# Softmax divisors of the last two head groups taken through small f32 matmuls, and the last quarter's output sums held open in PSUM

## The chip, the cores and the metric

The kernel runs on one core of a Trainium2 chip. The core has five engines with instruction streams of their own: TensorE (PE in the profile; PEld is its weight loads), VectorE (DVE), ScalarE (ACT), GpSimd (POOL) and SyncE (SP), which issues the DMAs. They meet through semaphores. The metric is the device time of one execution in microseconds: 742.52 us for the kernel before, the median of three runs (740.91 to 743.12).

## The reference

One sequence of S = 2048 tokens of width D = 640 is layer-normalized. On the result, multi-query attention (H = 32 query heads of width 20, one shared key and value head) and a feed-forward network (width F = 1728, silu) run side by side; their sum is added to the input.

```python
xn = _layernorm(x)                                    # x: [1, 2048, 640] bf16
q = (xn @ wq) -> [B, H, S, 20];  k = xn @ wk;  v = xn @ wv
p = softmax(einsum("bhqd,bkd->bhqk", q, k) * 20 ** -0.5)
att = einsum("bhqk,bkd->bhqd", p, v) -> [B, S, 640] @ wo
ffn = silu(xn @ w1) @ w2
return x + att + ffn
```

## The kernel before

**Tiling.** The queries are taken in four quarters of 512 (`QC`), the heads in eight groups of four (`HG`), which makes 32 groups in all, numbered 0 to 31; groups 24 to 31 are the last quarter. A group works on 16 key tiles of 128. One score tile (one key tile, one head, 512 queries) is one PE matmul on one of four row groups (L894) into one PSUM bank. There are 2048 of them. Most are exponentiated on ACT, two or three banks in one instruction (L978, 671 instructions). The rest go in batches of four heads to DVE, which builds an approximate exponential out of integer arithmetic: one conversion per head (L1155, 576) and two shifts per batch (L1188).

**Values and divisors.** The exponentials are multiplied with `v_all` by four matmuls, one on each of four column groups of PE ("a set", L1010), into bank 7 (`UB`). Each head has 32 rows there: 20 of output and, in row 20, the softmax divisor, which comes from a constant column in `v_all`. When a group is done, bank 7 is copied to `U_sb` (L1056 on DVE; for group 31 on ACT in two halves, L1067). For groups 0 to 29, `norm_job` then spreads the 4x512 divisors by DMA to 128x16, inverts them on DVE (L717), spreads the result by further DMAs over the rows of each head, multiplies on POOL (L725) and packs the heads into `oT` by DMA.

**The last two groups** (30 and 31) have no time for DMAs. There `sum_job` multiplies `U_sb` by a selection matrix `sel_f`, which repeats each head's divisor over its 32 rows (an f32 matmul, L838), DVE inverts all 128 rows (L841) and multiplies (L843). Their output rows stay in the padded layout of 32 rows a head, and `wo_end` holds the matching rows of `wo`. `make_sel` builds `sel_f` on POOL in a slot of `qT` that is free after group 22.

**Output.** The out projection and the second FFN product of a tile of 128 tokens and half the width (320) accumulate in one bank: 14 FFN chunks and five chunks of `oT`, each a set of four matmuls on column groups (`col_mm`, L379). For the last quarter this is split. `y_job` does the FFN part early, for token tiles 2 and 3 with the first three chunks of `oT` (`YC`), and evicts with the residual to `yx` (L783). For tiles 0 and 1, `ya_job` does those three chunks as a sum of its own, evicted onto `yx` by DVE (L794). At the end eight `fin_job`s (four tiles, two halves: "fins") take the fourth chunk and group 30 ("finA"), then group 31 ("finB", `fin_b`), and DVE writes the result (L823), which is stored by a DMA per token tile (L753).

**Order.** The program is written out by a planner, not by hand. `build` keeps a clock for every engine with estimated costs, commits one operation after another, and `emit` turns the order of each engine into its instruction stream with the semaphore waits. So the order is fixed; what takes longer on the chip than in the plan makes the engine wait. A DMA's estimate is its size argument divided by 250 bytes per ns, behind the DMAs already under way (`Sched.commit`). Side work for PE stands in two lists: `misc`, in order, paced by `misc_total` against the progress of the attention, and `misc_front`, which goes first. `next_misc` takes from `misc_front` only its first entry. A fin may start when no `y` or `ya` is left in `misc` and group 30 is divided.

**Head.** The 16 tiles of x are loaded by `load_x` (L405), in order with `wk`, the first columns of `wq`, `wv` and the rest of `wq`. DVE takes statistics (L484, L486), POOL the power -0.5 (L493), DVE or POOL normalizes (L509, L506), PE transposes (L516), and keys (L542), values (L566) and queries (L589) follow. For tiles 6 and 7 ACT takes the statistics (L473, L475). The first exponential needs the keys of tile 0 and the queries of tiles 0 to 3.

Of the kernel before, what the change touches and what calls it, by code (L numbers as in the profile page):

```python
# [14 lines left out]
P = 128  # L15
# [58 lines left out]
YA = 3  # L74
# [194 lines left out]
def build(nc, A_x, A_wq, A_wk, A_wv, A_wo, B_x, B_w1, B_w2, out, stack):  # L269
# [41 lines left out]
    sel_f = qT[:, 2, 0:2 * P].bitcast(F32)  # L311
# [9 lines left out]
    rS = Rrep  # L321
# [18 lines left out]
    h0f = hT[0][:, :, :].rearrange("p a b -> p (a b)")  # L340
    yx = h0f[:, 0:2 * QTP * D].bitcast(F32).rearrange("p (t d) -> p t d", t=QTP)
# [61 lines left out]
    def load_x(n):  # L403
        r = [res("xres", n)] if n < QTP else []
        x_ld[n] = dma(f"x{n}", lambda e, n=n: e.dma_start(x_home[n], xv[:, n, :]), P * D * 2,  # L405
                      writes=[res("xr", n)] + r)
# [39 lines left out]
    d_wv = dma("wv", lambda e: e.dma_start(wv_sb[:, :, 0:DH], wrow(A_wv)), P * DC * 256, writes=[res("wv")])  # L446
    d_wq = dma("wq", lambda e: e.dma_start(wq_sb[:, :, :], wrow(A_wq)), D * D * 2, writes=[res("wqs")])
# [342 lines left out]
    def ya_job(qc, i, hf):  # L790

        e0, e1 = hf * HALF, (hf + 1) * HALF
        job = pe_job(f"ya{qc}_{i}_{hf}", o_mms(qc, i, e0, e1, True, True, range(YA)), YA * 140)
        op = Op("dve", lambda v: v.scalar_tensor_tensor(out=yx[:, i, e0:e1], in0=bk(job.bank, 0, HALF), scalar=0.5,  # L794
                                                        in1=yx[:, i, e0:e1], op0=ALU.mult, op1=ALU.add),
                t_dve(HALF), 140, pre=[job.ready, y_op[(i, hf)]], reads=[], writes=[res("yx", i, hf)], prio=0.3, job=job)
        y_op[(i, hf)] = op
        job.consumers = [op]
        return job

# [4 lines left out]
    def fin_job(qc, i, hf):  # L805
        e0, e1 = hf * HALF, (hf + 1) * HALF
        mms = o_mms(qc, i, e0, e1, True, False, range(YA, DC - 1))

        def fa(pe, b):
            return col_mm(pe, b, e1 - e0, oT[:, 1 - qc % 2, 1, i * P:(i + 1) * P], wo_end[:, 0, e0:e1], False, False)  # L810
        mms.append((fa, t_mc(e1 - e0), "p", [oT_op[(1, 0)]] + d_wo_end, [res("oT", "end", 1, 0)]))
        job = pe_job(f"fin{qc}_{i}_{hf}", mms, len(mms) * 140)
        job.ready = None
        n = QTP * qc + i
        sl = n % 3 if n < NT - 1 else "x"

        def com(op):
            if (qc, i, 0) in half_op and (qc, i, 1) in half_op:
                store(qc, i)
        args = dict(pre=[y_op[(i, hf)]] + ([y_op[(0, 0)], y_op[(0, 1)]] if sl == "x" else []), reads=[res("yx", i, hf)],  # L820
                    writes=[res("os", sl) if hf == 0 else res("os2", sl)] + ([res("xres", 0)] if sl == "x" else []), prio=0.3, job=job, on_commit=com)
        dst = stage(n)[:, e0:e1]
        op = Op("dve", lambda v: v.scalar_tensor_tensor(out=dst, in0=bk(job.bank, 0, HALF), scalar=0.5, in1=yx[:, i, e0:e1],  # L823
                                                        op0=ALU.mult, op1=ALU.add), t_dve(HALF), 140, **args)
        op.gate = lambda: job.ready is not None and (sl not in store_op or store_op[sl].done or (qc, i, 1 - hf) in half_op)
        op.on_commit = lambda o: (half_op.__setitem__((qc, i, hf), op), com(o))
        job.consumers = [op]
        fin_made[(i, hf)] = job
        return job
# [3 lines left out]
    def sum_job(g, lo, hi, uc, rd):  # L833

        us, e, n = g % 2, NGR - 1 - g, hi - lo

        def f(pe, b):
            return pe.matmul(bk(b, 0, n), sel_f, U_sb[:, us, lo:hi], start=True, stop=True)  # L838
        job = pe_job(f"sum{g}", [(f, 4 * n / 2.4, "f", [uc] + sel, rd)], 500)
        rw = [res("Rrep", h) for h in range(HG)]  # L840
        r = Op("dve", lambda v: v.reciprocal(rS[:, lo:hi], bk(job.bank, 0, n)), t_dve(n), 140, pre=[job.ready], writes=[res("rS", k) for k in range(lo * 2 // QW, hi * 2 // QW)] + (rw if e else []),  # L841
               prio=0.1, job=job)
        op = dve(lambda v: v.tensor_tensor(oT[:, 0, e, lo:hi], U_sb[:, us, lo:hi], rS[:, lo:hi], ALU.mult), t_dve(n), 140,  # L843
                 pre=[r] + [out_done[(QC - 2, t)] for t in range(QTP)], reads=rd + [res("rS", k) for k in range(lo * 2 // QW, hi * 2 // QW)], writes=[res("oT", "end", e, lo)], prio=0.1)
        job.consumers = [r]
        oT_op[(e, lo)] = op
        return job
# [198 lines left out]
    def end_group(g, pv):  # L1046
# [8 lines left out]
        if g < NGR - 1:  # L1055
# [3 lines left out]
            if g < NGR - 2:  # L1059
                norm_job(g, uc)  # L1060
            else:
                misc_front.append(("sum", g, 0, QW, uc, [res("U", us)]))
            return
        h = QW // 2
        for k in range(2):
# [3 lines left out]
            misc_front.insert(k, ("sum", g, lo, hi, uc, [res("Uh", k)]))  # L1069
        for f in fins:  # L1070
            if f not in fin_asked:
                misc_front.append(("finA", qc) + f)
            misc_front.append(("finB", qc) + f)
# [187 lines left out]
    def make_sel():  # L1261
        v = sel_f.rearrange("p (i r) -> p i r", r=SLOT)
        a = pool(lambda g: g.memset(sel_f, 0.0), 180, writes=q_res[NGR - NQ] + [res("sel")], prio=0.91)
        sel.append(pool(lambda g: g.affine_select(out=v, in_=v, compare_op=ALU.not_equal, fill=1.0, base=-DH,
                                                  pattern=[[-SLOT, HG], [0, SLOT]], channel_multiplier=1), 280, pre=[a],
                        reads=[res("sel")], writes=[res("sel")], prio=0.92))
# [9 lines left out]
    def fill_misc():  # L1276
# [17 lines left out]
        for i in range(QTP):  # L1294
            for hf in range(2):
                if YC[i] < YA:
                    misc.append(("ya", QC - 1, i, hf))

    fill_misc()
    COST = {"q": 1.1, "h": 1.2, "out": 2.7, "y": 2.2, "ya": 0.5}  # L1300
# [20 lines left out]
    MAKE = {"q": q_job, "h": h_job, "out": out_job, "y": y_job, "ya": ya_job, "sum": sum_job, "finA": fin_a, "finB": fin_b}  # L1321

    def ready_to_make(m):
        if m[0] == "out":
            return (m[1], NG - 1) in pack_op and (m[1], m[2]) in xres_op
        if m[0] == "ya":
            return (m[2], m[3]) in y_op and all((m[1], g) in pack_op for g in range((YA * P - 1) // (HG * DH) + 1))
        if m[0] == "sum":
            return all((QC - 2, t) in out_done for t in range(QTP))
        if m[0] == "finA":  # L1330
            return (m[2], m[3]) in y_op and not any(isinstance(x, tuple) and x[0] in ("y", "ya") or isinstance(x, Piece) for x in misc) and all((m[1], g) in pack_op for g in range(NG - 2)) and (1, 0) in oT_op
        if m[0] == "finB":
            return (m[2], m[3]) in fin_made and len(oT_op) == 3
# [50 lines left out]
    def next_misc():  # L1384
# [3 lines left out]
        for q, src, ahead in ((misc_front, "front", 1), (misc, "misc", 16)):  # L1388
# [390 lines left out]
```

## Time and profile before

| what | us |
|---|---|
| median of three runs | 742.52 (740.91 to 743.12) |
| profiled execution, its own time | 744.36 |
| its span | 742.50 |
| first exponential on ACT starts | 14.23 |
| last exponential on ACT ends | 727.10 |
| last matmul set of bank 7 for group 31, end of its step in the chain | 727.88 |
| divisors of group 31 inverted on DVE (two instructions of 128x256) | 729.08 to 732.45 |
| last output half evicted by DVE | 739.71 to 740.20 |
| ACT busy in the span | 710.6 (96%) |
| PE busy / DVE busy in the span | 709.3 (96%) / 659.2 (89%) |

The span reaches from the first to the last instruction of the profiled execution; that execution's own time is 1.86 us longer, and was not one of the three runs of the median. "Busy" counts instructions in work, and matmul ends are modelled, so a busy PE may still wait. In a table of stages each line has the stage, its length, then for PE, PEld, DVE, ACT and POOL the busy time and the number of instructions, and at the end the granted clock of PE, the DMA share and GB/s. In a timeline a line has the start, the length, the engine, the source line, the operation with its form (out<-in), the count and, in brackets, the engine's idle time before it with what ended it.

### The profile page before, as it was taken

How to read it: one execution, taken by the hardware profiler on the slowest of the kernel's cores; microseconds unless marked ns; L12 is line 12 of the kernel's file. 1: busy time of each engine (PE TensorE's matmuls, PEld its weight loads, DVE VectorE, ACT ScalarE, POOL GpSimd, SP SyncE). 2: the span in 40 equal slices, each digit the busy share in tenths (PEclk: the TensorE clock that was granted, in tenths of full speed). 3: DMA queues.
4: the chain of work that ended last, by engine and by line, in shares of the span. 5: the costliest groups of instructions: out<-in, count | busy, mean ns of one | idle time of the engine just before them, and what ended most of it. 6: DMA issues, size and time to landing. Idle time of an engine off the chain costs nothing.

```text
span 742.5 us, 22537 instructions
## 1 busy us (share of the span) xinstructions
PE 709.3 (96%) x9922; PEld 236.7 (32%) x9925; DVE 659.2 (89%) x1144; ACT 710.6 (96%) x745; POOL 62.4 (8%) x72
## 2 busy tenths in 40 slices
PE   7999999999999999999999999999999999999986
PEld 5422222222223333222223333322223333333333
DVE  7779999999999489899998997999989968798985
ACT  6999999999999999999999999999999999999892
POOL 5500000000010000000000000000000000000000
PEclk9999999999999999999999999999999999999999
DMA  8812211222221122322111222122222211232201
GB/s 215 300 28 26 19 17 22 29 28 28 18 19 24 30 29 30 68 29 25 18 14 26 32 30 33 19 64 25 28 21 20 27 18 20 39 56 22 18 5 37
DMA packets 34160, 28.89 MB, mean 39 GB/s; under 512 B 15470, under 2 KB 29582, under 8 KB 34062
## 3 DMA queue, kind: packets, MB, share of 16 engines
q1 hardware_dynamic: 34062, 27.45, 23.9%
q8 instruction: 78, 1.28, 0.7%
q14 instruction: 20, 0.16, 0.1%
HBM read 11.01 MB, written 2.62 MB: 18 GB/s over the span
## 4 chain that ended last, share of the span: by engine, by line
ACT 62%; PE 23%; DVE 11%; SPq 1%; DMA 1%; issue 1%; POOL 0%; DVEq 0%; POOLq 0%
ACT sbt L978 60%; PE psall L894 8%; PE psall L1010 7%; PE psall L379 7%; DVE sbt L1155 4%; DVE sbt L1188 3%; ACT sbt L655 2%; DVE sbt L841 1%; SPq L626 1%; DMA sbt<-in_A_x_dram 1%; PE psall L1433 1%; DVE sbt L658 1%; DVE sbt L486 0%; DVE sbt L484 0%; DVE sbt L823 0%
## 5 line engine op out<-in xcount | busy, mean ns | idle before, releaser
L978 ACT ACTIVATE sbt<-psall 128x1024 bf16<-128x1024 f32 (+1 forms) x671 | 685.9, 1221 | 10.7 <-PE psall L894 10.4
L1155 DVE TENSOR_SCALAR sbt<-psall 128x512 int16<-128x512 f32 x576 | 373.0, 679 | 13.6 <-PE psall L894 10.3
L894 PE MATMUL psall<-sbt 32*128 32x512 bf16 x2048 | 279.6, 385 | 14.4 <-ACT sbt L978 6.1
L1010 PE MATMUL psall<-sbt 128*32 128x512 bf16 x3200 | 254.3, 386 | 3.9 <-DVE sbt L1056 3.4
L379 PE MATMUL psall<-sbt 128*32 128x320 bf16 (+1 forms) x3944 | 242.9, 334 | 5.8 <-DVE sbt L841 1.9
L1188 DVE TENSOR_SCALAR sbt<-sbt 128x2048 int16<-128x2048 int16 x288 | 199.5, 709 | 15.9 <-PE psall L1010 15.2
L894 PEld LDWEIGHTS psall<-sbt 32*128 32x128 bf16 x2048 | 73.1, 91 | 265.9 <-ACT sbt L978 182.9
L379 PEld LDWEIGHTS psall<-sbt 128*32 128x32 bf16 x3944 | 86.2, 96 | 99.2 <-issue 58.2
L1010 PEld LDWEIGHTS psall<-sbt 128*32 128x32 bf16 x3200 | 66.2, 95 | 112.3 <-issue 74.6
L725 POOL TENSOR_TENSOR sbt<-sbt 128x512 bf16<-128x512 f32 x30 | 40.9, 1364 | 620.9 <-DVE sbt L1155 216.4
L658 DVE SCALAR_TENSOR_TENSOR sbt<-sbt,psall 128x512 bf16<-128x512 bf16 (+1 forms) x56 | 37.9, 676 | 2.9 <-ACT sbt L655 1.8
L655 ACT ACTIVATE sbt<-psall 128x512 bf16<-128x512 f32 (+1 forms) x56 | 39.2, 701 | 0.3 <-PE psall L379 0.3
L1433 PE MATMUL psall<-sbt 128*32 128x512 bf16 (+1 forms) x512 | 34.9, 353 | 1.2 <-DVE sbt L408 1.2
L768 DVE SCALAR_TENSOR_TENSOR sbt<-psall,sbt 128x320 bf16<-128x320 f32 x24 | 11.7, 488 | 25.0 <-PE psall L379 24.9
L1056 DVE COPY sbt<-psall 128x512 f32<-128x512 f32 x31 | 21.1, 681 | 0.4 <-PE psall L1010 0.3
L613 DVE TENSOR_SCALAR sbt<-psall 128x512 bf16<-128x512 f32 x20 | 13.6, 679 | 4.4 <-PE psall L379 4.3
L1433 PEld LDWEIGHTS psall<-sbt 128*32 128x32 bf16 x512 | 13.3, 104 | 12.0 <-issue 6.6
L516 PE MATMUL psall<-sbt 128*128 128x128 bf16 x80 | 7.5, 221 | 2.3 <-DVE sbt L509 1.7
L506 POOL TENSOR_SCALAR sbt<-sbt 128x640 bf16<-128x640 bf16 x10 | 9.0, 910 | 3.0 <-DVE sbt L498 2.4
L841 DVE RECIPROCAL sbt<-psall 128x256 f32<-128x256 f32 (+1 forms) x3 | 6.7, 2267 | 2.2 <-PE psall L838 2.2
L783 DVE SCALAR_TENSOR_TENSOR sbt<-psall,sbt 128x320 f32<-128x320 f32 x8 | 3.9, 485 | 5.2 <-PE psall L379 5.1
L484 DVE BATCH_NORM_STATS2 sbt<-sbt 128x6 f32<-128x320 bf16 x14 | 6.5, 470 | 2.0 <-DMA sbt<-in_A_x_dram 1.9
(53 smaller groups left out, 86.3 us busy)
## 6 DMA issues: line engine op xcount, KB each, us to landing
sbt<-sbt SPq DMA_DIRECT2D x120, 64.0 KB, 3.8
sbt<-in_A_x_dram SPq DMA_DIRECT2D x28, 160.0 KB, 3.4
sbt<-sbt SPq DMA_DIRECT2D x213, 20.0 KB
out_dram<-sbt SPq DMA_DIRECT2D x16, 160.0 KB, 1.9
sbt<-in_B_w_dram SPq DMA_DIRECT2D x1, 2160.0 KB, 11.7
sbt<-in_B_w_dram SPq DMA_DIRECT2D x1, 2080.0 KB, 15.6
sbt<-sbt SPq DMA_DIRECT2D x75, 8.0 KB
sbt<-in_A_wq_dram SPq DMA_DIRECT2D x1, 800.0 KB, 7.1
```

Source lines behind the costliest of these rows:

```text
L379: ins = pe.matmul(ps[j * SLOT:(j + 1) * SLOT, b * BANK:b * BANK + n], w[:, j * SLOT:(j + 1) * SLOT], x, start=start, stop=stop, tile_posit ...
L655: t = Op("act", lambda a: a.activation(t_buf[0:rows, ts, :], bk(job.bank, 0, QW, rows=rows), AF.Tanh, scale=0.5), t_act(512), 215, pre=[jo ...
L658: u = Op("dve", lambda v: v.scalar_tensor_tensor(out=hT[par][0:rows, fk, :], in0=t_buf[0:rows, ts, :], scalar=1.0, in1=bk(job.bank, 0, QW, ...
L725: nm = pool(lambda e: e.tensor_tensor(oU[:, us, :], U_sb[:, us, :], Rrep, ALU.mult), 1700, pre=[uc] + lc, reads=[res("U", us)] + [res("Rre ...
L841: r = Op("dve", lambda v: v.reciprocal(rS[:, lo:hi], bk(job.bank, 0, n)), t_dve(n), 140, pre=[job.ready], writes=[res("rS", k) for k in ra ...
L894: return pe.matmul(bk(b), kT_rep[i * SLOT:(i + 1) * SLOT, kt * P:(kt + 1) * P], qT[i * SLOT:(i + 1) * SLOT, g % NQ, :], start=True, stop=T ...
L978: return a.activation(Ebuf[:, es * QW:es * QW + w], ps[:, buf[0] * BANK:buf[0] * BANK + w], AF.Exp, scale=ESCALE)
L1010: ins = pe.matmul(ps[i * SLOT:(i + 1) * SLOT, UB * BANK:UB * BANK + QW], lhsT, rhs, start=(first and k < HG), stop=(last and k >= len(lst) ...
L1056: uc = Op("dve", lambda v: v.tensor_copy(U_sb[:, us, :], bk(UB)), t_dve(512), 140, pre=[pv] + up, reads=[sc.banks[UB]], writes=[res("U", u ...
L1155: p1 = Op("dve", lambda v: v.tensor_scalar(z16[:, i * QW:(i + 1) * QW], bk(job.bank), ZBIAS, 0.0, ALU.add, ALU.max), t_dve(QW), 140, pre=[ ...
L1188: op = dve(lambda v, t=t, j=j: v.tensor_scalar_add(t[:, :].bitcast(I16), z16, float(SHIFT[j])), t_dve(N, 4), prio=3.0 - 0.01 * j, **args)
L1433: ins = pe.matmul(ps[i * SLOT:(i + 1) * SLOT, UB * BANK:UB * BANK + n], zero_t[:, 0:SLOT], zero_t[:, 0:n], start=fresh, stop=fresh, tile_p ...
```

## The change

Three things change.

1. For groups 30 and 31 the divisors are inverted in a narrow layout. `sum_job` makes four f32 matmuls, one for each 128 queries, with `U_sb` as the weights and a selection matrix of four columns (`sel4`) as the moving operand: 128 queries lie on the partitions, and the divisors of all four heads and four query tiles fill 128x16. DVE inverts these into `rLg`. The new `spread_job` brings them back: for each query tile and head one f32 matmul on one of the four column groups, with one column of `rLg` repeated 32 times as weights and an identity matrix (`ident_e`) as the moving operand. DVE multiplies `U_sb` by the result in PSUM. For group 31 the spread and the product come in two halves of 256 queries. `make_sel` builds both matrices in the same slot.
2. `ya_job` is gone. The fins take all chunks of `oT` that their `y` left out (`range(YC[i], DC - 1)`): four for token tiles 0 and 1, one for tiles 2 and 3. The last two fins (`LATE`) wait for both halves of group 31, `misc_front` is searched 20 entries deep, and finB follows directly behind its finA in that list. A branch with an eviction on ACT and an addition on POOL is there too, but `FIN_ACT` is empty, so it is not used.
3. The size arguments of the first loads in the planner (not the DMAs themselves) are set one by one: x4 counts as 612500 bytes, x5 to x7 as 75000, x8 to x15 as 107500 (163840 before), `wv` as 25000 (163840 before) and `wq` as 475000 (819200 before).

```diff
-YA = 3
+LATE = 2
+FIN_ACT = ()
+T_SUM = 110.0
+T_SPREAD = 230.0
...
-    sel_f = qT[:, 2, 0:2 * P].bitcast(F32)
+    sel4 = qT[:, 2, 0:2 * HG].bitcast(F32)
+    ident_e = qT[:, 2, QW - 2 * P:QW].bitcast(F32)
...
-        x_ld[n] = dma(f"x{n}", lambda e, n=n: e.dma_start(x_home[n], xv[:, n, :]), P * D * 2,
+        x_ld[n] = dma(f"x{n}", lambda e, n=n: e.dma_start(x_home[n], xv[:, n, :]), P * D * 2 if n < 4 else 612500 if n == 4 else 75000 if n < 8 else 107500,
...
-    d_wv = dma("wv", lambda e: e.dma_start(wv_sb[:, :, 0:DH], wrow(A_wv)), P * DC * 256, writes=[res("wv")])
-    d_wq = dma("wq", lambda e: e.dma_start(wq_sb[:, :, :], wrow(A_wq)), D * D * 2, writes=[res("wqs")])
+    d_wv = dma("wv", lambda e: e.dma_start(wv_sb[:, :, 0:DH], wrow(A_wv)), 25000, writes=[res("wv")])
+    d_wq = dma("wq", lambda e: e.dma_start(wq_sb[:, :, :], wrow(A_wq)), 475000, writes=[res("wqs")])
...
-    def ya_job(qc, i, hf):
...
-        mms = o_mms(qc, i, e0, e1, True, False, range(YA, DC - 1))
+        mms = o_mms(qc, i, e0, e1, True, False, range(YC[i], DC - 1))
...
-    def sum_job(g, lo, hi, uc, rd):
...
-            return pe.matmul(bk(b, 0, n), sel_f, U_sb[:, us, lo:hi], start=True, stop=True)
-        job = pe_job(f"sum{g}", [(f, 4 * n / 2.4, "f", [uc] + sel, rd)], 500)
...
-        r = Op("dve", lambda v: v.reciprocal(rS[:, lo:hi], bk(job.bank, 0, n)), t_dve(n), 140, pre=[job.ready], ...
+    def sum_job(g, ucs):
+
+        us = g % 2
+        mms = []
+        for t in range(QTP):
+            uc, rd = ucs[t * len(ucs) // QTP]
+
+            def f(pe, b, t=t):
+                return pe.matmul(bk(b, t * HG, (t + 1) * HG), U_sb[:, us, t * P:(t + 1) * P], sel4, start=True, stop=True)
+            mms.append((f, T_SUM, "f", [uc] + sel, [rd]))
+        job = pe_job(f"sum{g}", mms, 500)
+        r = Op("dve", lambda v: v.reciprocal(rLg[:, us, :], bk(job.bank, 0, QTP * HG)), 230, 140, pre=[job.ready],
+               writes=[res("rLg", us)], prio=0.1, job=job, name="recip")
...
+    def spread_job(g, lo, hi, ucs):
+
+        us, e = g % 2, NGR - 1 - g
+        mms = []
+        for t in range(lo // P, hi // P):
+            def f(pe, b, t=t):
+                for j in range(HG):
+                    w = rLg[:, us, t * HG + j:t * HG + j + 1]
+                    ins = pe.matmul(ps[j * SLOT:(j + 1) * SLOT, b * BANK + t * P:b * BANK + (t + 1) * P],
+                                    bass.AP(rLg, w.offset, [list(w.ap[0]), [0, SLOT]]), ident_e, start=True, stop=True,
+                                    tile_position=(0, j * SLOT))
+                return ins
+            mms.append((f, T_SPREAD, "f", [recip_op[g]] + sel, [res("rLg", us)]))
+        job = pe_job(f"spread{g}", mms, 500)
+        if not e and lo == 0:
+            job.fixed = UB
+        rd = [ucs[t * len(ucs) // QTP][1] for t in range(lo // P, hi // P)]
+        op = Op("dve", lambda v: v.tensor_tensor(oT[:, 0, e, lo:hi], U_sb[:, us, lo:hi], bk(job.bank, lo, hi), ALU.mult), t_dve(hi - lo), 140,
...
+        head = [("sum", g, ucs), ("spread", g, 0, h, ucs), ("spread", g, h, QW, ucs)] + list(misc_front)
+        head += [("finA", qc) + f for f in fins if f not in fin_asked]
...
+    def soon(op):
+        return op.done and op.fin + LAT <= sc.t["pe"] + 60.0
...
+        if m[0] == "spread":
+            return m[1] in recip_op and soon(recip_op[m[1]])
...
-        for q, src, ahead in ((misc_front, "front", 1), (misc, "misc", 16)):
+        for q, src, ahead in ((misc_front, "front", 20), (misc, "misc", 16)):
```

## The prediction

> **What bounds the kernel now.** I read the page's busy shares first, then the table of stages, then the tail and the head instruction by instruction.
>
> ```profile
> PE 709.3 (96%) x9922; PEld 236.7 (32%) x9925; DVE 659.2 (89%) x1144; ACT 710.6 (96%) x745; POOL 62.4 (8%) x72
> ...
> 14.23:40.00 25.77, 24.22 (x316) 11.33 (x321) 17.96 (x65) 24.10 (x23) 12.90 (x16) 1.00 0.77 244
> ...
> 200.00:300.00 100.00, 98.81 (x1469) 33.72 (x1466) 83.99 (x141) 99.96 (x104) 7.14 (x5) 1.00 0.21 27
> ...
> 728.30:732.40 4.10, 2.24 (x28) 1.13 (x28) 3.32 (x3) 0.26 (x1) 0.00 (x0) 1.00 0.00 0
> 732.40:735.70 3.30, 3.20 (x52) 2.04 (x56) 2.35 (x7) 0.00 (x0) 0.00 (x0) 0.53 0.00 0
> 735.70:738.60 2.90, 2.76 (x76) 1.85 (x68) 1.87 (x5) 0.00 (x0) 0.00 (x0) 0.95 0.05 15
> ```
>
> Between the first exponential (14.23) and the end of the last (727.10) ACT is the limit (99.96 of 100.00 us in one stage), with PE close behind. The 15.4 us after 727.10 are a chain of other engines, and there the change lies. In the table the granted clock is the third number from the end: 0.53 from 732.40 to 735.70, after a stage in which PE had work for 2.24 of 4.10 us.
>
> The tail, from the timeline (start, length, engine, line, form, count, idle before):
>
> ```profile
> 725.30 2.56 PE L1010 MATMUL psall<-sbt 128*32 128x512 bf16 x44
> 728.34 1.13 PE L838 MATMUL psall<-sbt 128*128 128x256 f32 x4 [0.49 <-ACT sbt L1067]
> 729.40 0.59 PE L379 MATMUL psall<-sbt 128*32 128x320 bf16 x12
> 730.89 0.59 PE L379 MATMUL psall<-sbt 128*32 128x320 bf16 x12 [0.90 <-DVE sbt L841]
> 732.50 5.95 PE L379 MATMUL psall<-sbt 128*32 128x320 bf16 x120 [1.02 <-DVE sbt L841]
> ...
> 729.08 3.37 DVE L841 RECIPROCAL sbt<-psall 128x256 f32<-128x256 f32 x2 [2.21 <-PE psall L838]
> 732.37 0.69 DVE L843 TENSOR_TENSOR sbt<-sbt 128x256 bf16<-128x256 f32 x2
> 732.97 1.84 DVE L794 SCALAR_TENSOR_TENSOR sbt<-psall,sbt 128x320 f32<-128x320 f32 x4
> 736.73 3.47 DVE L823 SCALAR_TENSOR_TENSOR sbt<-psall,sbt 128x320 bf16<-128x320 f32 x8 [1.91 <-PE psall L379]
> ```
>
> PE stands idle during the two reciprocals, then does 30 of its 36 four-matmul sets, mostly at half clock. The page's chain agrees: DVE L841 is 3.38 us of it, PE L379 4.61.
>
> The head (the same view, DVE and ACT):
>
> ```profile
> 7.52 0.43 DVE L509 TENSOR_SCALAR sbt<-sbt 128x640 bf16<-128x640 bf16 x1
> 9.16 0.94 DVE L486 BATCH_NORM_STATS2 sbt<-sbt 128x6 f32<-128x320 bf16 x2 [1.20 <-DMA sbt<-in_A_x_dram]
> 10.01 0.79 DVE L509 TENSOR_SCALAR sbt<-sbt 128x640 bf16<-128x640 bf16 x2
> ...
> 10.03 0.74 ACT L473 ACTIVATE sbt<-sbt 128x640 bf16<-128x640 bf16 x1 [0.82 <-DMA sbt<-in_A_x_dram]
> ...
> 14.23 6.94 ACT L978 ACTIVATE sbt<-psall 128x1536 bf16<-128x1536 f32 x6 [0.52 <-PE psall L894]
> ```
>
> DVE waits 1.20 us for x4 and x5 while the normalization of x2 and x3 (L509), whose factor POOL had at 8.51, stands behind them in its queue.
>
> **The change, part by part.**
>
> *Inversion of group 31, on the path.* Gone: four f32 passes (two matmuls), two reciprocals of 128x256 (3.37). Added: four f32 matmuls with U as weights and 4 columns, one reciprocal of 128x16 (0.24 us, row L717), 16 f32 matmuls of 128 columns with 32-column weights; the products read PSUM (as L593 does, 0.41, against 0.39).
> Prices: an f32 matmul is two passes; 256 columns take (1.13-0.71)/2 = 0.21 us a pass (0.71 is the chain's value for the first two), so 128 columns 0.107. The first two passes hold 0.71-2x0.21 = 0.29 beyond streaming; a four-matmul set's drain is 0.59-3x0.138 = 0.18, leaving 0.11 for a weight load. The sums, with 4 columns, are loads: 8x0.11 = 0.88. Bounds: 0.44 if half the loads are covered, 1.51 with each load at its full record (0.189); I take 0.88, as the view has such loads at that spacing.
> No row shows f32 matmuls on four column groups. Four abreast, as L379's, make 4x2x0.107 = 0.86 us for all 16; one after another 3.42. I take 1.71: PE issues in order, so the second pass of one group holds back the next group's first, but overlaps its second.
> The Trainium skill, page TensorEngine Tiling (Array Packing), section Tiling Modes (Key Properties), says that tiles operate independently and can load weights and multiply in parallel. By that the spreads would cost 0.86, and the sum below would be 0.85 us better; the L379 rows bear it out for bf16 only.
>
> *The `ya` jobs folded into the fins.* Their four f32 evictions (L794, 1.84 us of DVE) go; the 12 sets stay, in the fins of rows 0 and 1, which become five sets each instead of two. Sets in all: 12+16+8 = 36 before, 4x5+4x2+8 = 36 after. At most six fins, each with a PSUM bank, are open before the last spread, and seven of the eight banks are free by then: banks suffice.
>
> *New tail as a sum.* A set costs (0.93-0.10)/6 = 0.138 (chain: L379 x24 in 0.93), a switch between kinds of matmul 0.10 (L1010 x4 takes 0.33, x16 0.98: 0.217 a set, 0.11 over). The sum's start stays at 728.34, since it follows the last copy of U (L1067). Then PE has 0.88 + 36x0.138 (4.97) + 1.71 + three switches 0.30 = 7.86 us, to 736.20. It isn't starved: the reciprocal is ready at 729.22+0.18+0.04+0.24+0.05 = 729.73, while the first fin (0.69) runs to 730.0, and 24 sets (3.3 us) need neither spread of group 31. DVE has 0.24+0.82+8x0.40 = 4.3 us, so PE ends last. After its last set: 0.18 drain, 0.04, 0.49 (L823), then 2.30 as now (last L823 ends at 740.20, span 742.50): 739.2, against 742.5. **Gain 3.3.** Bounds by the spreads' price alone: 1.6 and 4.15; a fin that slips into PE's idle 0.66 us before 728.34 adds up to 0.66. What ends last then is PE, no longer DVE's reciprocal.
> This sum has PE at full clock. The row before the half clock is PE with 2.24 us of 4.10; the new tail has no gap over 0.5. If the sums' four columns count as idleness, half a clock for the 3.4 us that the present one lasts costs 1.7.
> The page TensorE: Matmul & The Clock Gate, Part 1, of the Trainium skill has the gate fall to half after an idle window of about 3.4 us. The trace agrees in level and length (0.53 over 3.30 us), though PE was not wholly idle before; by it this tail stays at full clock.
>
> *Inversion of group 30, at 713.57.* The same work, off the end's path: DVE loses 3.35 us (128x512) and gains 0.24; ACT ran without a gap from 715.06 to 727.09, so the saving is hidden. PE pays: 0.88+1.71+0.2 for 1.12, less the 0.66 us it stood idle behind L841. PE has no slack in 720.00:727.10 (7.10 of 7.10) and ends its last PV 0.8 us after the last exponential. Between 0 (spreads abreast) and 1.0: **loss 0.4**.
>
> *Selection matrix.* POOL clears 128x512 instead of 128x256 and runs one affine_select more (0.3 each): POOL is busy 8%, and the matrix is needed six groups later. Nothing, covered by that distance.
>
> *Load times in the ordering.* No DMA is added, and the sync queue's order of loads is the same; only the planner's landing times change. Planned x4 moves to about where the trace has it (first used at 9.16), so L509 should stand ahead of the wait, at 8.56 instead of 10.01. That is up to 1.45 us for what follows, but ACT has its own statistics of x6 and x7 from 10.03 on and is idle only 0.52 before 14.23. Earlier exponentials also meet the second key block (idle 0.49 at 22.15). From 0 to 1.45: **gain 0.6**, near ACT's own idle time.
>
> *The middle.* All orders are planned anew from 0 us on, and dropping `ya` alters the share of side work that paces the plan. One DVE batch (4 heads) more or less moves 4x0.45-0.47 = 1.9 us of ACT (a three-bank exponential takes 12.03/9 = 1.34). Another half-clock stretch at 688 now costs ACT 0.89+0.33. I take 0, bounds -2.5 and +2.5.
>
> Sum: -3.3+0.4-0.6 = -3.5. The profiled execution took 744.36 (span 742.50), 1.84 over the median 742.52; taken off the median, **739.0**.
>
> **The rivals.**
> B: better still. Spreads abreast (4.15), group 30 free, the head's full 1.45 or the stretch at 688 gone (1.2): up to 742.5-4.15-0.66-1.45-1.2 = 735.0. For it: the bf16 sets do run abreast. Against: everything must fall well.
> C: no difference that shows. Spreads one after another and the head unchanged: 742.5-1.6+1.0 = 741.9; or full half clock: 739.0+1.7 = 740.7. For it: no row of f32 on column groups. Against: even serial spreads cost no more than the reciprocals that go.
> D: slower. The replanned middle gives DVE fewer batches: each costs ACT 1.9, so from three fewer of the 144 (5.7: 744.7) the change loses; four give 746.6. For it: DVE is full in some stages (98.72 of 100), and the plan is greedy, so small edits move everything. Against: DVE has only lost work.
> E: the ordering's new times do nothing for the head (x4's statistics still ahead): 739.6. It stays inside the forecast.
>
> **How the numbers follow.** A measurement of this kernel tells about 0.3% (2.2 us) from none. Forecast with E, 737.3 to 740.3: 0.46. B, 735.0 to 737.3: 0.22. C with small losses of the middle, 740.3 to 744.7: 0.20. D: 0.12. Faster is 0.46+0.22 = 0.68. The range 735.3 to 742.4 holds the forecast, nearly all of B (0.20) and the greater part of C (0.15).
>
> **What would show it.** From the end of the last exponential to the end: 15.4 us now, about 12.1. No reciprocal of 128x256 or 128x512, 32 of 128x16. Granted clock near 1.00 in the tail; no idle time of PE over 0.6 after 728. No 320-column f32 evictions but eight. DVE's wait for x4 behind L509, and that at about 8.6. I am wrong if f32 matmuls of one column group follow another with 0.2 us each, if the tail falls to half clock, or if the exponentials on ACT (671) or DVE's 576 conversions change by more than a batch or two.

## The result and the profile after

The changed kernel takes 745.06 us (median of 19 runs, 742.97 to 746.94), the kernel before, in the same runs, 742.52 us. The ratio is 1.0036, with a 95% interval of 1.0022 to 1.0051: a little slower, where a gain of 3.5 us was forecast. The 739.0 us and the whole range (735.3 to 742.4) lie below it.

The two profiled executions must be read with care. That of after took 743.95 us, near the lower end of its kernel's times; that of before took 744.36, near the upper end of its own. So their spans are alike (742.2 and 742.5) though the kernels are not. What they show well is where the time lies. Cut at the start of the first and the end of the last exponential on ACT:

| part of the span, us | before | after | difference | forecast |
|---|---|---|---|---|
| head: start to first exponential | 14.23 | 13.71 | -0.5 | -0.6 |
| middle: first to last exponential | 712.87 | 717.12 | +4.25 | 0, bounds -2.5 and +2.5, with +0.4 for group 30 |
| tail: last exponential to the end | 15.40 | 11.32 | -4.1 | -3.3 |

The tail did more than was forecast. The middle took it back. First the page of after: busy times, then the groups of the exponentials and of DVE's conversions (count, busy time, mean ns, idle time before them and what ended it).

```profile
PE 713.7 (96%) x10076; PEld 240.8 (32%) x10079; DVE 658.5 (89%) x1145; ACT 710.8 (96%) x740; POOL 62.3 (8%) x73
...
L1010 ACT ACTIVATE sbt<-psall 128x1024 bf16<-128x1024 f32 (+1 forms) x666 | 685.5, 1239 | 13.6 <-PE psall L926 13.0
L1193 DVE TENSOR_SCALAR sbt<-psall 128x512 int16<-128x512 f32 x580 | 374.3, 680 | 16.0 <-PE psall L926 13.4
```

The page of before has these two groups:

```profile
L978 ACT ACTIVATE sbt<-psall 128x1024 bf16<-128x1024 f32 (+1 forms) x671 | 685.9, 1221 | 10.7 <-PE psall L894 10.4
L1155 DVE TENSOR_SCALAR sbt<-psall 128x512 int16<-128x512 f32 x576 | 373.0, 679 | 13.6 <-PE psall L894 10.3
```

The exponentials cost ACT the same, 685.5 against 685.9 us, and DVE has one batch more (580 conversions against 576), not less. What grew is ACT's idle time, by 2.9 us in this group: it waits for score matmuls (10.4, now 13.0 us). Over all of ACT's instructions the gaps of the middle grew from 10.69 to 14.85 us, which is 4.16 of its 4.25. The table of stages shows it as well; after the stage and its length come busy time and count for PE, PEld, DVE, ACT and POOL, the granted clock, the DMA share and GB/s. First the stage from 500 to 600 of before, then three stages of after:

```profile
500.00:600.00 100.00, 97.98 (x1318) 30.14 (x1314) 89.48 (x151) 99.67 (x110) 7.58 (x7) 1.00 0.22 24
```

```profile
200.00:300.00 100.00, 97.77 (x1444) 33.72 (x1441) 83.81 (x141) 98.84 (x100) 5.76 (x5) 1.00 0.21 27
500.00:600.00 100.00, 95.69 (x1280) 28.68 (x1272) 93.88 (x158) 96.77 (x106) 6.19 (x8) 0.98 0.22 22
...
730.84:742.20 11.36, 8.30 (x224) 6.31 (x216) 5.19 (x12) 0.66 (x2) 0.00 (x0) 1.00 0.17 61
```

ACT has 98.84 of 100 us where it had 99.96, and 96.77 from 500 to 600, where before has 99.67. (That stage of after holds a stretch of half clock, at 566.04; the middle of before has one too, at 688.20, so the two middles differ by something else.) The last line is the new tail: clock 1.00, where before had 0.53 in one stage of it. Instruction by instruction (start, length, engine, line, form, count, idle before; without PEld, one eviction of the FFN part and the stores):

```profile
731.34 0.66 ACT L1102 ACTIVATE sbt<-psall 128x256 f32<-128x256 f32 x2 [0.50 <-PE psall L1042]
732.17 1.05 PE L848 MATMUL psall<-sbt 128*128 128x4 f32 x8
733.15 0.87 PE L383 MATMUL psall<-sbt 128*32 128x320 bf16 x20
733.26 0.26 DVE L851 RECIPROCAL sbt<-psall 128x16 f32<-128x16 f32 x1 [0.48 <-PE psall L848]
733.85 1.04 PE L865 MATMUL psall<-sbt 128*32 128x128 f32 x32
734.53 0.86 DVE L874 TENSOR_TENSOR sbt<-sbt,psall 128x256 bf16<-128x256 f32 x2 [1.02 <-PE psall L865]
734.72 4.42 PE L383 MATMUL psall<-sbt 128*32 128x320 bf16 x124
735.77 1.45 DVE L827 SCALAR_TENSOR_TENSOR sbt<-psall,sbt 128x320 bf16<-128x320 f32 x3 [0.37 <-PE psall L383]
737.54 2.32 DVE L827 SCALAR_TENSOR_TENSOR sbt<-psall,sbt 128x320 bf16<-128x320 f32 x5 [0.33 <-PE psall L383]
```

From 732.17 PE has no idle time: sums (L848), five sets of fins, the spreads (L865), 31 more sets, to 739.14. These are 6.97 us, where the sum forecast 7.86 and 0.18 of drain.

### The profile page after: what moved, and what is told of

It is laid out like the page before. It is cut to its first block, busy times and chain, and to the rows that moved or that the text cites. A ratio compares the mean times of both kernels' runs of the same rounds, so it can differ in the third digit from the quotient of the medians.

```text
span 742.2 us, 22840 instructions
## 1 busy us (share of the span) xinstructions
PE 713.7 (96%) x10076; PEld 240.8 (32%) x10079; DVE 658.5 (89%) x1145; ACT 710.8 (96%) x740; POOL 62.3 (8%) x73
## 4 chain that ended last, share of the span: by engine, by line
ACT 48%; PE 31%; DVE 18%; DMA 1%; SPq 1%; issue 1%; POOL 0%; DVEq 0%
ACT sbt L1010 46%; PE psall L926 11%; PE psall L383 10%; DVE sbt L1193 9%; PE psall L1042 9%; DVE sbt L1226 5%; ACT sbt L659 2%; PE psall L1472 1%; DVE sbt L662 1%; DVE sbt L488 1%; SPq L630 1%; DMA sbt<-sbt 1%; DVE sbt L1088 0%; DVE sbt L490 0%; DMA sbt<-in_A_x_dram 0%
## 5 line engine op out<-in xcount | busy, mean ns | idle before, releaser
L1010 ACT ACTIVATE sbt<-psall 128x1024 bf16<-128x1024 f32 (+1 forms) x666 | 685.5, 1239 | 13.6 <-PE psall L926 13.0
L383 PE MATMUL psall<-sbt 128*32 128x320 bf16 (+1 forms) x3944 | 238.1, 333 | 1.0 <-DVE sbt L1193 0.7
L1226 DVE TENSOR_SCALAR sbt<-sbt 128x2048 int16<-128x2048 int16 x290 | 202.9, 717 | 10.8 <-PE psall L1042 10.3
L1472 PE MATMUL psall<-sbt 128*32 128x512 bf16 (+1 forms) x584 | 38.5, 352 | 1.2 <-DVE sbt L412 1.2
L721 DVE RECIPROCAL sbt<-sbt 128x16 f32<-128x16 f32 x30 | 7.3, 242 | 0.3 <-DMA sbt<-sbt 0.3
```

Of the source, the lines that this page charges most:

```text
L383: ins = pe.matmul(ps[j * SLOT:(j + 1) * SLOT, b * BANK:b * BANK + n], w[:, j * SLOT:(j + 1) * SLOT], x, start=start, stop=stop, tile_posit ...
L1010: return a.activation(Ebuf[:, es * QW:es * QW + w], ps[:, buf[0] * BANK:buf[0] * BANK + w], AF.Exp, scale=ESCALE)
L1226: op = dve(lambda v, t=t, j=j: v.tensor_scalar_add(t[:, :].bitcast(I16), z16, float(SHIFT[j])), t_dve(N, 4), prio=3.0 - 0.01 * j, **args)
L1472: ins = pe.matmul(ps[i * SLOT:(i + 1) * SLOT, UB * BANK:UB * BANK + n], zero_t[:, 0:SLOT], zero_t[:, 0:n], start=fresh, stop=fresh, tile_p ...
```

## The experiments

Two theories stood after the result. One: the tail gains, and the replanned middle lost by chance, as any other small edit might. The other: the new load times themselves make a worse middle. In the edits below "old load times" means the size arguments of the kernel before:

```diff
-... P * D * 2 if n < 4 else 612500 if n == 4 else 75000 if n < 8 else 107500,
+... P * D * 2,
-... wrow(A_wv)), 25000, writes=[res("wv")])
-... wrow(A_wq)), 475000, writes=[res("wqs")])
+... wrow(A_wv)), P * DC * 256, writes=[res("wv")])
+... wrow(A_wq)), D * D * 2, writes=[res("wqs")])
```

and "old pace" restores the share by which side work is paced, which dropping the four `ya` entries at 0.5 had altered:

```diff
-    misc_total = sum(COST[m[0]] for m in misc)
+    misc_total = sum(COST[m[0]] for m in misc) + 2.0
```

All ratios are against the kernel before on the same chip, with 95% intervals.

**Tail alone, on the order of before.** The changed kernel with old load times and old pace. PE's order is then that of before up to the sums of group 30, close to the end.

> The changed kernel with the load times of before and the pace of before (the total of side work counts 2.0 more, as with the four ya jobs), so that PE's order is that of before up to group 30's sum. Theory (the new tail gains 4.1 us between the last exponential and the end, 15.4 to 11.3, and the 4.25 us that the middle lost come from the new plan): middle from first to last exponential 712.9 again within 1.5, time 738 to 739.5, ratio 0.993 to 0.996. Rival 1 (the new inversion of group 30 and the held banks make the middle longer): middle 715 or more, ratio 0.999 or more.

Measured: 736.86 us against 741.77, 0.9923 [0.9895, 0.9951]. The execution that was profiled took 1142.61 us, with ACT waiting for 340 us of it, and tells nothing of the tail, so the same kernel ran again:

> The kernel of the first experiment again (new tail, load times and pace of before), for a profile of it without a disturbance. Theory (the tail's gain is real and lies behind the last exponential): time 736 to 738.5; from the last exponential to the end 11 to 12 instead of 15.4, granted clock 1.00 there. Rival (the first measurement was luck): 740 or more.

Measured: 738.1 against 742.08, 0.9946 [0.9927, 0.9965]. The profile has a tail of 11.18 us, 4.2 less than before's 15.40. So the tail is worth 4 to 5 us when nothing else moves.

**Tail alone, replanned.** Old load times, the changed kernel's pace.

> As the run before, but with the pace of the changed kernel (2.0 less side work in the total); orders part about half way. Theory (any new plan draws the middle anew): tail 11.3, middle differs from 712.9 by more than 1 us in either direction, gaps of ACT other than before's. Rival 2 (the load times alone lengthen the middle): middle 712.9 within 1, time as the run before, 738 to 739.5.

Measured: 739.47 against 741.77, 0.9965 [0.9948, 0.9983]. Here PE's order leaves that of before about half way. More side work is left for the end (behind the first copy of group 31 stand 53 sets of output matmuls, in before 36; tail 13.54), the middle is shorter (709.03), and the kernel still wins.

**Load times alone.** The kernel before, with nothing but the new size arguments.

> The kernel before with the new load times in the planner alone. Theory: first exponential at 13.7 instead of 14.2, tail 13.8 to 15.4, middle drawn anew: time 740 to 747. Rival 2: middle 717 as in the changed kernel, time 745 to 747.

Measured: 749.65 against 741.77, 1.0098 [1.0069, 1.0126]. Seven to eight us are lost by an edit that adds no instruction to the tail, which keeps its wide reciprocals. The middle takes 720.5 us. The tail takes 11.59, not the 13.8 to 15.4 that were expected, though its two reciprocals last 3.37 us as before: only 16 sets are left for the end, the rest stands ahead. So middle and tail trade work from plan to plan, and a tail prices the inversion only where the order is that of before (the runs above and the two at the end of this section).

**The change with the old pace.** Only the `misc_total` line above.

> The changed kernel with the pace of before; its PE order is the changed kernel's for the first 460 of 1622 rows, then another. Theory: tail 11.3, first exponential 13.7, middle other than 717.1 by over 1 us. Rival 2: middle 717 again, time 745.

Measured: 747.48, 1.0067 [1.0043, 1.0091]; middle 719.5. The old pace doesn't bring the time back.

**Other plans of the same work.** To tell a bad draw from a bad rule, both kernels (old and new load times) were replanned with a constant of the planner moved by a nanosecond, one of them at a time, up (as here) or down (69 and 104). `LAT` is the delay that the planner puts between one engine's end and another's start, `SWITCH` its price for PE's change from one kind of matmul to another:

```diff
-LAT = 70.0
+LAT = 71.0
-SWITCH = 105.0
+SWITCH = 106.0
```

> New tail, old load times, and one constant of the planner nudged by 1 ns (LAT 70 to 71), so that the plan parts from the others after about a tenth of PE's order while nothing else changes. Theory (every new plan draws the middle at random): time anywhere from 736 to 746, and the four runs of this call overlap between old and new load times. Rival 2 (the new load times themselves make the middle longer): 735 to 740, below both runs with new load times by 4 us or more.

> The changed kernel with LAT 71 instead of 70. Theory: 736 to 748, other than 745 by over 1.5. Rival 2: 744 to 749, above both runs with old load times.

> New tail, old load times, the planner's SWITCH 106 instead of 105 ns. Theory: 736 to 746. Rival 2: 735 to 740.

> The changed kernel with SWITCH 106. Theory: 736 to 748. Rival 2: 744 to 749.

> New tail, old load times, LAT 69 instead of 70. Theory (plans fall by chance, whatever the load times): as likely above as below the runs with new load times, 736 to 750. Rival 2 (the new load times lengthen the middle): 736 to 741.

> The changed kernel with LAT 69. Theory: 736 to 750. Rival 2: 744 or more.

> New tail, old load times, SWITCH 104 instead of 105. Theory: 736 to 750. Rival 2: 736 to 741.

> The changed kernel with SWITCH 104. Theory: 736 to 750. Rival 2: 744 or more.

All plans that have the new tail. "Planned" is the end of the order by the planner's own clock, the latest end among its operations; the last four columns are from one profile each (start of the third exponential, copy of group 0 out of bank 7, middle, tail). The us are medians; the ratio is the one on record and not the quotient of two medians.

| load times, plan | us | ratio | planned | third exp. | group 0 | middle | tail |
|---|---|---|---|---|---|---|---|
| old, order of before | 738.1 | 0.9946 [0.9927, 0.9965] | 734.1 | 16.38 | 48.6 | 711.4 | 11.2 |
| old, new pace | 739.47 | 0.9965 [0.9948, 0.9983] | 735.0 | 15.30 | 47.5 | 709.0 | 13.5 |
| old, SWITCH 106 | 739.27 | 0.9986 [0.9963, 1.0009] | 732.1 | 15.50 | 47.8 | 707.9 | 13.5 |
| old, LAT 69 | 739.8 | 0.9987 [0.9968, 1.0006] | 732.8 | 16.02 | 48.5 | 708.5 | 14.0 |
| old, SWITCH 104 | 741.38 | 0.9996 [0.9980, 1.0012] | 734.6 | 15.80 | 48.3 | 715.2 | 9.9 |
| old, LAT 71 | 748.70 | 1.0111 [1.0089, 1.0134] | 745.1 | 18.43 | 50.6 | 719.2 | 13.9 |
| new, the change itself | 745.06 | 1.0036 [1.0022, 1.0051] | 737.4 | 16.27 | 48.9 | 717.1 | 11.3 |
| new, SWITCH 104 | 743.67 | 1.0024 [1.0002, 1.0045] | 733.1 | 16.57 | 51.6 | 714.8 | 10.6 |
| new, LAT 69 | 745.7 | 1.0054 [1.0036, 1.0071] | 738.8 | 16.74 | 54.8 | 721.2 | 10.3 |
| new, old pace | 747.48 | 1.0067 [1.0043, 1.0091] | 742.5 | 16.20 | 49.1 | 719.5 | 10.5 |
| new, LAT 71 | 747.95 | 1.0099 [1.0069, 1.0129] | 740.5 | 16.70 | 50.1 | 719.2 | 11.1 |
| new, SWITCH 106 | 751.88 | 1.0149 [1.0113, 1.0185] | 745.4 | 16.95 | 55.9 | 726.8 | 12.3 |

Chance is large: a constant moved by 1 ns moves the time by up to 9.2 us at the same load times (739.47 to 748.70; with the new ones from 745.06 to 743.67 on one side and 751.88 on the other). But the two groups also differ. The mean ratio of the six old-load plans is 0.9997 (with the mean of 0.9923 and 0.9946 for the first), of the six new-load plans 1.0072: 0.75%, or 5.6 us. Of the six pairs with the same constants and pace, the new load times are slower in five, by 0.28 to 1.63%, and faster in one (LAT 71, by 0.12%). That is less than it seems, since plans with neighbouring constants share much of their order and are no independent draws.

**What the plans say of themselves.** The order is fixed before anything runs, and with it the planned end (`build` of a kernel file, called by itself, gives it without a chip). For the kernel before it is 734.6 us, for the change 737.4, for the load times alone 741.1. Over the twelve plans it goes with the measured ratio (correlation 0.90). The last copy of group 31 ends at 724.0 in the plan of before and at 727.0 in that of the change, 3.0 later; in the two profiles it ends at 728.56 and 732.00, 3.4 later. So most of what the middle lost was already in the order as the planner itself had priced it, and could be read without a run. The gain of the tail could not: the plan gives the tail alone 0.5 us of its 4.

The planned end can also be had for constants that never ran on the chip. With the new tail and pace, and LAT between 60 and 80 or SWITCH between 99 and 111, 29 settings in all, it is 740.8 on average with the old load times (732.1 to 751.4) and 738.6 with the new ones (729.7 to 748.0); the new ones end later in 11 of the 29. In the five settings of the table they do on average, 739.0 against 735.9. So, as far as the plan can tell, the new load times make no worse orders as a rule: near the kernel's own constants the old ones happen to plan well, and the new ones don't. These are estimates of the planner; what the chip would make of the other settings was not run.

**Where the plans with the new load times lose.** Two places show, and a remainder doesn't. The first is the head. DVE in the profile of the tail alone, replanned (old load times):

```profile
8.78 0.79 DVE L513 TENSOR_SCALAR sbt<-sbt 128x640 bf16<-128x640 bf16 x2
...
10.40 0.87 DVE L532 COPY sbt<-psall 128x640 bf16<-128x640 bf16 x2
11.19 0.41 DVE L597 TENSOR_SCALAR sbt<-psall 128x256 bf16<-128x256 f32 x1
...
11.90 0.42 DVE L597 TENSOR_SCALAR sbt<-psall 128x256 bf16<-128x256 f32 x1
```

and in the profile of the change, which differs from it in the load times alone:

```profile
8.85 0.80 DVE L513 TENSOR_SCALAR sbt<-sbt 128x640 bf16<-128x640 bf16 x2 [0.59 <-POOL sbt L497]
...
10.75 0.48 DVE L532 COPY sbt<-psall 128x640 bf16<-128x640 bf16 x1
11.14 0.41 DVE L597 TENSOR_SCALAR sbt<-psall 128x256 bf16<-128x256 f32 x1
11.47 0.48 DVE L532 COPY sbt<-psall 128x640 bf16<-128x640 bf16 x1
...
11.99 0.44 DVE L490 BATCH_NORM_STATS2 sbt<-sbt 128x6 f32<-128x320 bf16 x1
...
12.78 0.42 DVE L597 TENSOR_SCALAR sbt<-psall 128x256 bf16<-128x256 f32 x1
```

The normalization L513 starts at the same time in both (8.78, 8.85), since x4 and x5 had landed early in the first. But with the new times DVE takes the transposes out of PSUM one at a time (L532, 10.75 and 11.47, against two from 10.40) and does further statistics before the second half of the queries (L597), which is ready 0.88 us later. The third exponential starts at 16.20 to 16.95 in the seven new-load profiles (those of the table and of the load times alone), against 15.30 to 16.54 in six old-load ones (those of the table and of before, without LAT 71, which has a stretch of half clock in the head); the medians are 16.57 and 15.91. Two more profiles with the head of before, from the end of this section, have 15.76 and 15.49, so one and the same order moves by about a microsecond from execution to execution. The new time of x4 fits one execution only: it plans the landing at 9.04, as in the profile of before (9.13), but in 15 of the 17 profiles x4 landed between 6.7 and 7.6, near the 7.24 of the old time.

The second place is group 0. Its copy comes at 48.8 to 55.9 (seven new-load profiles, mean 51.3), against 47.5 to 50.6 (seven old-load ones with that of before, mean 48.6). For the two latest there is a likely reason: in six of the seven new-load profiles PE's matmuls or weight loads for scores wait between 20 and 60 us for a DMA from SBUF to SBUF, which lays out queries; in none of the seven old-load ones do they. The wait is long in the two whose group 0 ends latest (3.0 us with SWITCH 106, 2.4 with LAT 69); in the other four it is 0.2 to 0.6, and the load times alone lose their seven us without it. The size arguments that changed add up to 751,620 bytes less, so by the planner's 250 bytes per ns its DMA queue comes free 3.0 us earlier, while the DMAs are what they were. In the plans the DMAs of the first two blocks of queries have landed by 39.3 us with the new load times and by 42.3 with the old; in the profile of SWITCH 106 PE's wait for them ended at 42.88. There the waits between 20 and 60 us are (us in total, times, longest):

```profile
ACT sbt L1010 <- PE psall L926: 8.3, 5, 5.6
DVE sbt L1193 <- PE psall L926: 6.0, 4, 4.5
...
PE psall L926 <- DMA sbt<-sbt: 2.7, 1, 2.7
```

and the timeline of it:

```profile
42.89 0.60 PE L926 MATMUL psall<-sbt 32*128 32x512 bf16 x1 [2.74 <-DMA sbt<-sbt]
...
47.21 1.45 ACT L1010 ACTIVATE sbt<-psall 128x1536 bf16<-128x1536 f32 x1 [5.56 <-PE psall L926]
```

PE waits for the queries, falls to half clock (a matmul of 512 columns takes 0.60 instead of 0.39), and ACT stands for 5.56 us. In the profile of the change itself the wait is 0.3 us only. There the loss lies later, and no single place has it: the copy of group 9 comes 2.2 us earlier than in the profile of before, that of group 11 5.3 later, of group 13 0.6 earlier, of group 26 7.6 later, of group 31 3.4 later. From group 0 to group 31 the old-load profiles take 674 to 686 us (mean 678.1), the new-load ones 677 to 686 (mean 682.7). These overlap, and no wait separates them. Why the planner's choices end later with just these numbers stays open.

**The two parts of the tail apart.** First the narrow inversion with `ya_job` and its entries in `misc` kept as before, and old load times; the order is that of before up to group 30.

```diff
+    def ya_job(qc, i, hf):
...
-        mms = o_mms(qc, i, e0, e1, True, False, range(YC[i], DC - 1))
+        mms = o_mms(qc, i, e0, e1, True, False, range(YA, DC - 1))
```

> Of the change only the narrow inversion (128x16 between two sets of f32 matmuls); the four ya jobs, the load times and the pace are those of before, and so is PE's order up to group 30's sum. Theory (the two reciprocals of 3.4 us and the half clock behind them are what the tail loses): most of the gain of the run before, time 736.5 to 739. Rival (the sums kept open bring it): 740 to 742.

Measured: 737.98 against 742.08, 0.9952 [0.9933, 0.9970]; tail 11.40. Next the open sums with before's inversion, load times and pace:

```diff
-    def ya_job(qc, i, hf):
...
-        mms = o_mms(qc, i, e0, e1, True, False, range(YA, DC - 1))
+        mms = o_mms(qc, i, e0, e1, True, False, range(YC[i], DC - 1))
...
+    misc_total = sum(COST[m[0]] for m in misc) + 2.0
```

> Of the change only the sums kept open (no ya jobs, fins of five sets for rows 0 and 1); inversion, load times and pace of before, PE's order the same as before throughout. Theory (the four evictions of 0.46 us were beside PE's work): 741 to 742.5, ratio 0.998 to 1.001. Rival: 737 to 739.

Measured: 740.34, 0.9980 [0.9963, 0.9997], below the 741 to 742.5 that were expected; tail 13.19. Its tail:

```profile
728.50 3.37 DVE L830 RECIPROCAL sbt<-psall 128x256 f32<-128x256 f32 x2 [2.20 <-PE psall L827]
728.83 0.87 PE L379 MATMUL psall<-sbt 128*32 128x320 bf16 x20
730.32 0.87 PE L379 MATMUL psall<-sbt 128*32 128x320 bf16 x20 [0.62 <-DVE sbt L830]
731.93 3.74 PE L379 MATMUL psall<-sbt 128*32 128x320 bf16 x104 [0.74 <-DVE sbt L830]
```

and as one stage of the table (the clock is the third number from the end):

```profile
726.50:739.70 13.20, 7.32 (x164) 4.41 (x156) 7.34 (x12) 0.68 (x3) 0.00 (x0) 1.00 0.14 51
```

Each wait for a reciprocal now covers five sets instead of three, PE's idle times there fall from 0.90 and 1.02 to 0.62 and 0.74, and the clock stays at 1.00. So folding `ya` alone gains 1.7 us; on top of the narrow inversion it gains nothing that shows (738.1 against 737.98), presumably since both take away the same idle time. The inversion alone brings all of the tail's gain.

## Why the prediction was wrong

The step that failed is "The middle", with "I take 0, bounds -2.5 and +2.5". In the profiles it was +4.25, and from plan to plan of the same work it spreads from 707.9 to 726.8 (in part because plans leave more or less for the end). The bounds were priced by one DVE batch and one half-clock stretch. Neither carries it: the batches rose by one, and the loss is ACT waiting for score matmuls that stand later in PE's order. The new order was longer by the planner's own clock, which put the last copy of group 31 3.0 us later; the prediction did not read it. Rival D had the right sign but the wrong mechanism: it had priced the loss by batches that DVE would lose. The chance of 0.12 was too low, because the plan was treated as something that an edit disturbs a little, while the twelve plans show that a nanosecond can be enough for nine us. Which way the draw fell was luck, as far as the 29 settings above can tell.

The head was "gain 0.6". The normalization (L509, L513 after) did move forward, to 8.85, and the idle time that the prediction read was real, but its size depends on the run: under the old order DVE waits until 9.45 in one profile (wait of 1.15 us) and not at all in another, as x4 and x5 land. What was missed is that the planner uses the new times for everything else too: the queries' evictions come later, and DMAs of query pieces are expected too early. The first exponential came 0.5 us earlier in the profile, and the third 0.27; over the profiles, the new load times lose at the third (medians 16.57 against 15.91). The 0.6 was worked out from one execution, in which x4 landed later than in all others.

The tail was right in its mechanism, and each term can be read above.

- The sums were 0.88: 1.05 with a drain of 0.18, so 0.87.
- The spreads were mis-sized: 1.71 was taken between 0.86 and 3.42; they take 1.04 with the drain, so 0.86. The column groups work abreast in f32 too, and issue in order does not hold them back. The prediction had beside this what the Trainium skill says on the page TensorEngine Tiling (Array Packing), section Tiling Modes (Key Properties), that tiles operate independently; the trace agrees, with 0.86 us for 32 passes of 128 columns.
- The reciprocal was 0.24 and takes 0.26. The clock stayed at 1.00 as forecast.
- 36 sets were to take 4.97: the two rows have 0.87 and 4.42, less 0.18 of drain each 4.93.
- After PE's last set 2.83 were forecast with the drain left out, and 3.02 passed.

Together 12.1 forecast, 11.32 measured in after and 11.18 in the tail alone: the 0.85 of the spreads is the difference, and the other terms cancel within 0.1.

Group 30 was to lose 0.4. From the copy of group 30 to that of group 31 it takes 18.92 us in before and in the open sums alone, and 18.52 in the two kernels with the narrow inversion on the same order: 0.4 less. But that is no gain of the inversion: only 120 matmuls of the 128x320 form stand between the two copies, where before has 136, since four sets have moved behind the second copy, into PE's idle time ahead of the sums. At 0.138 each they are 0.55, and without them group 30 loses 0.15. The prediction's own terms with the spreads abreast give 0.88+0.86+0.2-1.12-0.66 = 0.16.

Folding `ya` was priced at nothing. That holds on top of the inversion; alone it gains 1.7 us, which the prediction did not ask for.

The best version is the change without its load times and with the old pace: 0.9946 and 0.9923 in two series, faster than both kernels. The narrow inversion alone, at 0.9952, can't be told from it.

## What to carry to other kernels

Where a planner writes the order, an edit is two edits: the work that it changes, and a new draw of the whole order, whose spread has to be measured (by constants moved a little) and put into the range. Read the planner's own end of the new order first: here it said 2.8 us longer before anything ran. Test a local gain with the old order kept up to the place; if it then shows, as the 4 us here, the plan is what has to be repaired. Times fitted to one profile aren't thereby truer, as x4 shows, and a planner that is given other times for a few transfers isn't thereby given a better order: what queues behind them moves as well.

## What the runs showed of the hardware

The half clock comes in stretches of 3.41 us, or of twice that (6.83 in the profile of SWITCH 106 with new load times), and they make up part of the spread of a kernel's runs. Of the 19 runs of the change, six of the eight with a mean granted clock of 1.0 took 742.97 to 743.56 us (the other two 744.57 and 745.91). The three with 0.993, which is what three such stretches make (half of 3 times 3.41 us is 0.7% of the time), took 746.65 to 746.78: some 1.1 us for each stretch. One of them in the profile of before, with the windows ahead of it (stage, length, busy times as above, clock):

```profile
684.80:688.20 3.40, 2.20 (x33) 0.67 (x29) 3.31 (x7) 3.40 (x5) 0.00 (x0) 1.00 0.02 6
688.20:691.60 3.40, 3.40 (x31) 0.88 (x34) 2.32 (x5) 2.51 (x3) 0.00 (x0) 0.50 0.02 2
```

PE had work for 2.20 of 3.40 us, and the clock was halved for the next 3.4, in which ACT has 2.51 instead of 3.40. The Trainium skill, page TensorE: Matmul & The Clock Gate, Part 1, has the gate fall after an idle window of about 3.4 us; length and level agree, but here the window was not idle. The share in work alone doesn't decide it: in the profile of the tail alone, which has the same order there, PE had work for 2.21 of the same 3.40 us and the clock stayed at 1.00, while in that of the change it fell after 2.63 of 3.40. Four profiles share one order from group 0 to the copy of group 30 (before, the tail alone and the two parts of the tail). Of their 30 steps from group to group 12 agree within 0.02 us; others differ by up to 1.3 us with no half clock in them. From group 0 to group 30 they take 658.91 us (with no such stretch) to 661.35 (with one). So these four executions of one order lie within 2.5 us, where the plans of the table differ by up to 13.8.

The landing of the first loads isn't steady either: x4 landed at 9.13 us in the profile of before, at 8.64 in that of LAT 71 with old load times, and between 6.7 and 7.6 in the 15 others. A gain read from a single profile's head can be that run's own.
